# A linear-attention and routed-experts kernel: the first batch in another order, the first two units' x sums in the dense blocks, the balancing in place

## The chip, the cores and the metric

The kernel runs on one core of a Trainium2 chip. Its engines work side by side, each through its own list of instructions in order: PE (TensorE, matmuls), DVE (VectorE), ACT (ScalarE), POOL (GpSimd) and SP (SyncE, which here only issues transfers). They meet through semaphores: an instruction that waits holds up all that stands behind it on its engine. The metric is the time of one execution on the device in microseconds (us), less is better.

## The reference

Eight batches of eight heads, 576 positions, 64 features, in float32. Attention is linear: queries and keys pass a relu and are doubled by a cosine and a sine of the position.

```python
def phi(x, c, s):
    r = np.maximum(x, 0.0)
    return np.concatenate([r * c, r * s], axis=-1)
q_p = phi(q, cos_w, sin_w)
k_p = phi(k, cos_w, sin_w)
kv = np.einsum('bhsf,bhsd->bhfd', k_p, v)
z = np.sum(k_p, axis=2)
num = np.einsum('bhsf,bhfd->bhsd', q_p, kv)
den = np.einsum('bhsf,bhf->bhs', q_p, z)[..., None] + 1e-06
```

The result num / den, as 4608 tokens of 512 features, is the x of a layer of 8 experts. The routing weights P are balanced by eight rounds over rows and columns, and every expert sees every token:

```python
P = np.exp(logits)
for _ in range(8):
    P /= P.sum(1, keepdims=True) + 1e-09
    P /= P.sum(0, keepdims=True) + 1e-09
    P *= N / E
for e in range(E):
    h = np.maximum(x @ w1[e], 0.0)
    out += P[:, e:e + 1] * (h @ w2[e])
```

## The kernel before

The kernel goes through four stages.

**Start and first batch (0 to about 25 us).** POOL issues the loads: queries of batch 0 in two halves (L244, L258), keys, values, the first expert's weights, then batch 1. Between the query loads POOL makes an index row (`iota`) and an identity matrix. From the index row ACT makes the table `cs` of cosines and sines. DVE writes constants, then scales the queries (`prep_q`), PE turns each of them by matmuls with the identity (`turn`), and ACT takes the result out of PSUM. Keys get a relu (`prep_k`), and the sums over positions of the scaled keys come from PE straight (`key_sums`) and go through DVE into `zsel` (`key_sums_made`). `prep_kp` scales keys. `denominators` makes q times z on PE for some heads; after the last head DVE takes the reciprocal and splits it into a high and a low half (`hi`, `hl`). `sums_begun` makes kv on PE, 36 matmuls for a half, `sums_made` copies it to `kv_sb` on ACT. `attend` then, for each of four head pairs (hk), spreads the reciprocals by matmuls (`rb`, copied by ACT), makes the numerators on PE, and DVE multiplies both into `xT`. Between the pairs stand the first matmuls of the first dense block (`first_ps`) and, at L669 to L674, relus and scaled keys of batch 1. `keep_busy(n)` puts n filler matmul blocks of 128 columns on PE.

**Blocks 0 to 6 (to about 165 us).** Tokens are taken in nine blocks of 512. Each has 16 slots: eight matmul groups with w1 (`ffn1`, relu into hT on ACT) and eight halves with w2 (`ffn2`). Into the slots a hand-written table (`at`) puts the attention of the next batches. In block 6, slots 1 and 8, `x_sums_early` makes the four sums of a unit of x (`x_sums`) for units 0 and 1, into buffers of the pool of `k_p`; SP stores three of them in DRAM.

**Blocks 7 and 8 (to about 189 us).** The last dense blocks of the first expert; H takes the place of hT and lies on memory that the attention stage gave back. The sums of units 0 and 1 are read again from DRAM (`x_again`, L1109). Here the balancing starts: `sinkhorn` is a generator, and `balanced(n)` takes n steps of it at given slots. Five steps make a round: row sums and reciprocal; product and column sums; two steps of the second expert's w1 sums (T); a matmul that adds the columns over partitions, and other T steps; reciprocal and the last scaling. Products go to a second buffer `P_exp` that lies expert by expert.

**Seven more experts (to the end).** Their products are made with 7 instead of 8 block products (Strassen's scheme in Winograd's form), on sums of x, w1 and H. A `group` makes four products with w1 for a unit of 2 x 384 tokens, a `Pair` those with w2. The first group loop (e = 1, n = 0) takes in the rest of block 8's `ffn2` and the rest of the balancing (`start_fill`).

What sets the order: `te`, `ve`, `se` are wrappers (InOrder) that keep each engine's instructions about as written; waits come from the tiles that they read and write.

Of the kernel before, what the change touches and what calls it, by code (L numbers as in the profile page):

```python
# [25 lines left out]
def kernel(  # L26
# [128 lines left out]
    def ffn2(hT, w, c0, g, y_ps, fts):  # L155
# [9 lines left out]
        if FT - 1 in fts:  # L165

            if g % 2 == 0 or g < B * TCH // P:
                se.copy(out=acc(g), in_=y_ps)
            else:
                ve.tensor_copy(out=acc(g), in_=y_ps)  # L170
# [9 lines left out]

    NT = N // 2
    TU = 3 * P
    NU = NT // TU
    KH = KT // 2
    FH = FT // 2
    UG = TU // P
    DH = Dm // 2

    def x_part(half, kh, n):
        t0 = half * NT + n * TU  # L190
        return xT[:, kh * KH : (kh + 1) * KH, t0 : t0 + TU]

    x_saved = dram.tile([NU, 3, P, KH * TU], F16, name="x_saved")

    def x_sums(n, ts):

        a11, a12, a21, a22 = (x_part(i, j, n) for i in range(2) for j in range(2))
        s1, s2, s4 = ts
        for out_, in0, in1, op in (
            (s1, a21, a22, ALU.add), (s2, s1, a11, ALU.subtract),  # L200
            (s4, a12, s2, ALU.subtract), (a21, a11, a21, ALU.subtract),
        ):
            ve.tensor_tensor(out=out_, in0=in0, in1=in1, op=op)
            yield
        for i, t in enumerate(ts):
            nc.sync.dma_start(out=x_saved[n, i], in_=t.rearrange("p k t -> p (k t)"))

    with ExitStack() as p1:
# [35 lines left out]
        load(0, 0, "q")  # L244
        gidx = cs_pool.tile([P, C], FP32, name="gidx")
# [4 lines left out]

        ones_sq = cs_pool.tile([P, P], F16, name="ones_sq")
# [6 lines left out]
        load(0, 1, "q")  # L258
        for name in "kv":
            load(0, 0, name)  # L260
            load(0, 1, name)
# [41 lines left out]
        for hh in range(2):  # L303
            ve.tensor_copy(
                out=cs_half[hh * HP : (hh + 1) * HP, :, :, hh],
                in_=cs[hh * HP : (hh + 1) * HP, :, :, 0],
            )
# [8 lines left out]
        C3 = C // 3  # L316

# [6 lines left out]
        with nc.allow_low_precision("sums of zeros and ones"):  # L324
# [11 lines left out]
        ones_col = const.tile([P, 1], FP32, name="ones_col")  # L336
        ve.memset(ones_col[:], 1.0)
        ones_all = const.tile([P, P], FP32, name="ones_all")
        ve.memset(ones_all[:], 1.0)
        eps_row = cs_pool.tile([1, 32], FP32, name="eps_row")  # L340
        ve.memset(eps_row[:], 1e-6 / XS)
# [8 lines left out]
        lent = acc_lo[:, G_LO - 4 : G_LO, :].rearrange("p g d -> p (g d)").bitcast(F16)  # L350
        VA = C * (D + 2)
        v_augs = [
            lent[:, i * VA : (i + 1) * VA].rearrange("p (c d) -> p c d", d=D + 2)
            for i in range(4)
        ]
# [7 lines left out]
        for t in v_augs:  # L363
            ve.memset(t[:, :, D : D + 1], 1.0 / XS)

# [107 lines left out]
        def sums_begun(b, half):  # L473
# [7 lines left out]
            kv_ps = [ps_s.tile([P, 512], FP32, name="small_ps") for hh in range(2)]  # L481
# [75 lines left out]

        def attend(b, hk):

            parts = ((0, 2 * C3), (2 * C3, C))  # L560
            rb_ps = [ps_s.tile([P, 512], FP32, name="small_ps") for _ in parts]
            rb = rb_pool.tile([P, C * HP], FP32, name="rb")
            for i, (c0, c1) in enumerate(parts):
# [8 lines left out]
                se.copy(out=rb[:, c0 * HP : c1 * HP], in_=rb_ps[i][:, 0 : (c1 - c0) * HP])  # L572
            num_ps = [ps_s.tile([P, 512], FP32, name="small_ps") for _ in parts]
# [48 lines left out]
        for hk in range(HK):  # L622
            if hk == 3:
                prep_k(0, 0)
                prep_k(0, 1)
                z_ps = key_sums(0)
                prep_q(0, hk)
                key_sums_made(0, z_ps)
            else:
                prep_q(0, hk)  # L630
            for i in range(3):
                turn(0, hk, i, True)
                keep_busy(3)
        prep_kp(0, 0)
        prep_kp(0, 1)
        denominators(0, range(0, 4))
        keep_busy(8)
        for hk in (2, 3):
            prep_k(0, hk)
        z_ps = key_sums(1)  # L640
        prep_kp(0, 2)
        key_sums_made(1, z_ps)
        prep_kp(0, 3)
        keep_busy(5)
        denominators(0, range(4, 8))
        for half in range(2):
            sums_made(0, half, sums_begun(0, half))
            keep_busy((0, 18)[half])
# [7 lines left out]
        for hk in range(HK):  # L656
            attend(0, hk)
            for kt in ((), (0,), (1,), (2, 3))[hk]:
                for ft, h_ps in enumerate(first_ps):
# [9 lines left out]
            for i in ((), (0,), (1, 2), ())[hk]:  # L669
                prep_k(1, i, i < 2)  # L670
            for i in ((), (0,), (1,), (2, 3))[hk]:
                if i == 3:
                    prep_k(1, i, False)
                prep_kp(1, i)  # L674
# [81 lines left out]
        def x_sums_early(n):  # L756
            ts = [kp_pool.tile([P, C, 2, D], F16, name="k_p") for _ in range(3)]
            for _ in x_sums(n, [
                t[:].rearrange("p c a d -> p (c a d)")[:, 0 : KH * TU].rearrange(
                    "p (k t) -> p k t", k=KH  # L760
                ) for t in ts
            ]):
                pass

        for n in range(2):
            at(B - 2, (1, 8)[n], x_sums_early, n)
# [490 lines left out]
```

## Time and profile before

| what | us |
|---|---|
| median of three executions | 979.27 (979.09 to 979.95) |
| the profiled execution, its own time | 979.95 |
| its span, first to last instruction | 978.2 |
| PE busy | 963.7 |
| DVE busy | 808.2 |
| ACT busy | 565.6 |
| POOL busy | 60.7 |

A line of the timeline has the start in us, the duration in us, the engine, the line of the program (L109 is the wrapper's line, so most instructions have it), the operation, what it writes <- what it reads, the shape, and how many like it stand together (x3; the duration is then that of all). In brackets stands how long the engine was idle before it, and what it waited for. A line of groups ends with busy time in us, mean of one in ns, and idle time before. A line of stretches is told where it is shown.

### The profile page before, as it was taken

What the parts mean: (1) busy time and instruction counts of PE and PEld (TensorE: products, weight loads), DVE (VectorE), ACT (ScalarE), POOL (GpSimd) and SP (SyncE); (2) the same over time, 40 slices, a digit from 0 to 9 for tenths busy, and PEclk for the clock granted to TensorE, in tenths of its full rate; (3) what the DMA queues carried; (4) which work ended last, traced back from release to release, by engine and by line L of the source; (5) the groups of instructions that cost most, each with busy time, mean ns of one, the idle gap of its engine ahead of it and who ended that gap; (6) DMA issues with size and microseconds to landing.
All of it is one profiled execution on the core that took longest, in us unless ns stands there. A gap on an engine that the chain in (4) does not pass through costs nothing.

```text
span 978.2 us, 20250 instructions
## 1 busy us (share of the span) xinstructions
PE 963.7 (99%) x7855; PEld 674.4 (69%) x7855; DVE 808.2 (83%) x1831; ACT 565.6 (58%) x1264; POOL 60.7 (6%) x82
## 2 busy tenths in 40 slices
PE   9999999999999999999999999999999999999997
PEld 6544454557777777777777777777777777777775
DVE  6767774888988888988888888988888888988887
ACT  5766665577776555555555555555555555555551
POOL 6231110010000000000000000000000000000001
PEclk9999999999999999999999999999999999999999
DMA  9999888140103401223103401223103401114435
GB/s 162 187 150 173 149 144 184 32 79 28 48 25 77 84 25 35 65 53 68 40 25 78 83 25 37 64 55 66 40 25 77 83 25 39 36 26 121 126 89 127
DMA packets 81200, 74.72 MB, mean 76 GB/s; under 512 B 33360, under 2 KB 73040, under 8 KB 81104
## 3 DMA queue, kind: packets, MB, share of 16 engines
q0 software_dynamic: 27232, 30.94, 20.6%
q1 hardware_dynamic: 53632, 42.24, 17.6%
q8 instruction: 61, 1.00, 0.4%
q14 instruction: 35, 0.29, 0.1%
q10 hardware_dynamic: 240, 0.26, 0.1%
HBM read 84.30 MB, written 12.98 MB: 99 GB/s over the span
## 4 chain that ended last, share of the span: by engine, by line
PE 93%; DMA 2%; DVE 2%; ACT 1%; POOL 1%; issue 1%; ACTq 0%; POOLq 0%; SPq 0%
PE rows_ps L109 34%; PE h_ps L109 28%; PE p_ps L109 11%; PE copied_ps L109 11%; PE y_ps L109 5%; PE small_ps L109 4%; DMA acc_hi<-q_p 1%; DMA k_ld<-in_k_dram 1%; DMA x_saved<-k_p 1%; ACT hT L109 0%; ACT acc_lo L109 0%; DVE acc_hi L939 0%; POOL hs_last L954 0%; DMA out_dram<-acc_lo 0%; DVE xT L109 0%
## 5 line engine op out<-in xcount | busy, mean ns | idle before, releaser
L939 DVE SCALAR_TENSOR_TENSOR acc_lo<-rows_ps,P_tok,acc_lo 128x512 f32<-128x512 f32 (+1 forms) x322 | 203.9, 643 | 74.9 <-PE rows_ps L109 74.8
L109 PEld LDWEIGHTS <-H 128*128 128x128 f16 x2080 | 203.2, 98 | 82.3 <-issue 1.2
L875 ACT CAST u<-h_ps 128x384 f16<-128x384 f32 x288 | 137.5, 478 | 131.2 <-PE h_ps L109 131.2
L109 PEld LDWEIGHTS <-w1e 128*128 128x128 f16 x1632 | 157.3, 98 | 68.1 <-issue 6.8
L869 DVE CUSTOM_DVE_ANT_0 H<-p_ps,u 128x384 f16<-128x384 f32 x329 | 181.9, 553 | 6.5 <-PE p_ps L109 6.5
L109 PEld LDWEIGHTS <-hs 128*128 128x128 f16 x1500 | 146.6, 98 | 56.2
L109 PE MATMUL p_ps<-xT,T 128*128 128x384 f16 x672 | 164.1, 326 | 1.2 <-DVE H L109 1.0
L109 PE MATMUL h_ps<-S,w1e 128*128 128x384 f16 x672 | 164.1, 326 | 0.6 <-ACT u L109 0.3
L109 PE MATMUL rows_ps<-V,H 128*128 128x256 f16 x1000 | 150.0, 273 | 0.7 <-DVE acc_hi L939 0.7
L109 PE MATMUL h_ps<-xT,w1e 128*128 128x384 f16 (+1 forms) x616 | 149.7, 350 | 0.8 <-ACT H L109 0.8
L109 PE MATMUL rows_ps<-w2e,hs 128*128 128x256 f16 x1000 | 150.0, 273 | 0.0
L907 ACT ACTIVATE H<-h_ps 128x384 f16<-128x384 f32 x144 | 70.6, 490 | 95.1 <-PE h_ps L109 95.1
L109 PEld LDWEIGHTS <-T 128*128 128x128 f16 x1008 | 98.4, 98 | 32.0 <-issue 5.4
L109 PE MATMUL rows_ps<-w2e,H 128*128 128x256 f16 (+1 forms) x568 | 92.5, 285 | 0.0
L888 ACT COPY copied_ps<-h_ps 128x384 f32<-128x384 f32 x144 | 67.5, 469 | 35.5 <-PE h_ps L109 35.5
L898 ACT ACTIVATE H<-copied_ps 128x384 f16<-128x384 f32 x144 | 70.8, 492 | 20.4 <-PE copied_ps L109 20.4
L109 PE MATMUL h_ps<-S,T 128*128 128x384 f16 x336 | 81.8, 324 | 0.6 <-ACT copied_ps L109 0.3
L109 PE MATMUL copied_ps<-xT,w1e 128*128 128x384 f16 x336 | 82.1, 326 | 0.0
L109 PE MATMUL copied_ps<-w2e,H 128*128 128x256 f16 x504 | 75.5, 272 | 0.0
L109 PE MATMUL rows_ps<-V,hs 128*128 128x256 f16 x500 | 75.0, 272 | 0.0
L939 DVE SCALAR_TENSOR_TENSOR acc_lo<-copied_ps,P_tok,acc_lo 128x256 f32<-128x256 f32 x126 | 60.4, 480 | 0.6 <-PE copied_ps L109 0.2
L939 DVE SCALAR_TENSOR_TENSOR acc_hi<-rows_ps,P_tok,acc_hi 128x512 f32<-128x512 f32 (+1 forms) x56 | 41.4, 739 | 20.5 <-PE rows_ps L109 19.7
(144 smaller groups left out, 952.6 us busy)
## 6 DMA issues: line engine op xcount, KB each, us to landing
S<-x_saved SPq DMA_DIRECT2D x114, 192.0 KB, 2.4
out_dram<-acc_lo SPq DMA_DIRECT2D x62, 128.0 KB, 2.4
w1e<-in_moe_w_dram POOLq DMA_DIRECT2D x7, 1024.0 KB, 9.2
w2e<-in_moe_w_dram POOLq DMA_DIRECT2D x7, 1024.0 KB, 9.6
q_ld<-in_q_dram POOLq DMA_DIRECT2D x16, 288.0 KB, 7.0
k_ld<-in_k_dram POOLq DMA_DIRECT2D x16, 288.0 KB, 8.2
v_ld<-in_v_dram POOLq DMA_DIRECT2D x16, 288.0 KB, 9.3
x_saved<-S SPq DMA_DIRECT2D x12, 192.0 KB, 1.8
```

The lines of the kernel that those rows point to most:

```text
L109: i = getattr(self.engine, name)(*args, **kwargs)
L869: latest = ve._custom_dve(TENSOR_ADD_SAT, out=out, in0=ps[:, 0:TU], in1=t[:], s0=FP32_MAX, s1=0.0)
L875: se.copy(out=t[:], in_=ps[:, 0:TU])
L888: se.copy(out=Y[:, 0:TU], in_=X[:, 0:TU])
L898: se.activation(out=h11, in_=Y[:, 0:TU], func=AF.Relu)
L907: se.activation(out=h12, in_=X[:, 0:TU], func=AF.Relu)
L939: ve.scalar_tensor_tensor(out=a, in0=rows, scalar=P_tok[:, g, self.e : self.e + 1], in1=a, op0=ALU.mult, op1=ALU.add,)
```

## The change

In the start, both query loads are issued first, the identity is made between the two key loads, and DVE's constants are written ahead of the queries' scaling; two copies for `cs_half` move behind two of the scaled queries (`halve`). All four queries are scaled ahead of the keys' relus. The scaled keys of pairs 2 and 3 move behind the reciprocals. `attend` is cut in `spread_out` and `numerators`; the second half of kv is made behind the first numerators, in the two banks of `h_ps`. The relus and scaled keys of batch 1 all come behind the last numerators, the two relus on ACT ahead of the first relus into hT.

`x_sums_early` goes. The sums of units 0 and 1 are made by DVE in blocks 7 and 8, in the tiles that the products read, and stored from there; they are not read again.

The balancing works in place in `P_tok`, token by token: product and last scaling write in one run, and the column sums read every eighth value. Its steps are dealt otherwise: 23 in the two blocks (28 before), 17 (12 before) in the first group. The 16 T steps go to rounds 1 to 4, four each. Of block 7's results two, tiles 29 and 31, are copied by DVE instead of ACT.

```diff
-            if g % 2 == 0 or g < B * TCH // P:
+            if g % 2 == 0 or g < (B - 1) * TCH // P:
                 se.copy(out=acc(g), in_=y_ps)
...
         load(0, 0, "q")
+        load(0, 1, "q")
         gidx = cs_pool.tile([P, C], FP32, name="gidx")
...
+        load(0, 0, "k")
         ones_sq = cs_pool.tile([P, P], F16, name="ones_sq")
...
-        load(0, 1, "q")
-        for name in "kv":
-            load(0, 0, name)
-            load(0, 1, name)
+        load(0, 1, "k")
+        for half in range(2):
+            load(0, half, "v")
...
         for hk in range(HK):
+            prep_q(0, hk)
+            if hk == 1:
+                halve()
             if hk == 3:
                 prep_k(0, 0)
                 prep_k(0, 1)
                 z_ps = key_sums(0)
-                prep_q(0, hk)
-                key_sums_made(0, z_ps)
-            else:
-                prep_q(0, hk)
             for i in range(3):
                 turn(0, hk, i, True)
                 keep_busy(3)
         prep_kp(0, 0)
+        key_sums_made(0, z_ps)
+        for hk in (2, 3):
+            prep_k(0, hk)
         prep_kp(0, 1)
         denominators(0, range(0, 4))
+        z_ps = key_sums(1)
         keep_busy(8)
+        key_sums_made(1, z_ps)
+        denominators(0, range(4, 8))
+        sums_made(0, 0, sums_begun(0, 0))
+        keep_busy(20)
         for hk in (2, 3):
-            prep_k(0, hk)
-        z_ps = key_sums(1)
-        prep_kp(0, 2)
-        key_sums_made(1, z_ps)
-        prep_kp(0, 3)
-        keep_busy(5)
-        denominators(0, range(4, 8))
-        for half in range(2):
-            sums_made(0, half, sums_begun(0, half))
-            keep_busy((0, 18)[half])
+            prep_kp(0, hk)
+        spread_out(0, 0)
+        numerators(0, 0)
+        keep_busy(8)
+        spread_out(0, 1)
+        sums_made(0, 1, sums_begun(0, 1, (ps_h[0], "h_ps")))
+        keep_busy(8)
...
         for hk in range(HK):
-            attend(0, hk)
+            if hk > 1:
+                spread_out(0, hk)
+            if hk:
+                numerators(0, hk)
+            if hk == 3:
+                prep_k(1, 0)
+                prep_k(1, 1)
             for kt in ((), (0,), (1,), (2, 3))[hk]:
-                for ft, h_ps in enumerate(first_ps):
+                for ft, h_ps in ((2, first_ps[2]), (3, first_ps[3]), (0, first_ps[0]), (1, first_ps[1])):
...
-            for i in ((), (0,), (1, 2), ())[hk]:
-                prep_k(1, i, i < 2)
-            for i in ((), (0,), (1,), (2, 3))[hk]:
-                if i == 3:
-                    prep_k(1, i, False)
-                prep_kp(1, i)
+        for hk in range(HK):
+            if hk >= 2:
+                prep_k(1, hk, False)
+            prep_kp(1, hk)
         for hk in range(3):
             prep_q(1, hk)
...
-        for n in range(2):
-            at(B - 2, (1, 8)[n], x_sums_early, n)
...
             ve.tensor_tensor(
-                out=P_exp[:].rearrange("p e c -> p c e"), in0=P_tok[:],
+                out=P_tok[:], in0=P_tok[:],
                 in1=rr[:].unsqueeze(2).to_broadcast([P, NG, E]), op=ALU.mult,
             )
...
-            ve.reduce_sum(out=colp[:], in_=P_exp[:], axis=AX.X)
+            ve.reduce_sum(
+                out=colp[:], in_=P_tok[:].rearrange("p c e -> p e c"), axis=AX.X
+            )
...
-                out=P_tok[:].rearrange("p c e -> p e c"), in0=P_exp[:],
+                out=P_tok[:], in0=P_tok[:],
                 scalar=float(N) / float(E) / (XS if it == 7 else 1.0),
-                in1=t2[:].unsqueeze(2).to_broadcast([P, E, NG]),
+                in1=t2[:].unsqueeze(1).to_broadcast([P, NG, E]),
...
-    tw_steps = [[steps_left.pop(0) for _ in range(n)] for n in (2, 3, 4, 3, 4, 0, 0, 0)]
+        tw, tw_steps[1 + i] = w1_steps(w_next, i)
...
-    for n in range(2):
-        x_again(n, xs_first[n])
+    sums_x = x_sums(0, xs_next)
...
-            balanced({1: 3, 4: 5, 8: 5, 13: 5, 17: 5, 22: 5}.get((j - B + 1) * NS + slot, 0))
+            if j == B - 1 and slot:
+                next(sums_x, None)
+            if j == NJ - 1:
+                if slot == 0:
+                    sums_x = x_sums(1, xs_first[1])
+                next(sums_x, None)
+            since = (j - B + 1) * NS + slot - 5
+            if since == -4:
+                balanced(3)
+            elif since >= 0 and since % 5 < 2:
+                balanced((1, 4)[since % 5])
...
-        balanced({3: 1, 4: 1, 5: 1, 6: 2, 11: 1, 12: 1, 13: 1, 14: 2, 19: 1, 20: 1}.get(k_fill, 0))
+        if k_fill % 6 != 1:
+            balanced(1)
```

## The prediction

> **What bounds the kernel now.** I read the page's header, busy line and slices, then busy time by stretches, then the timelines of the two places that the change touches: the first batch (0 to 35 us) and the dense blocks with the Sinkhorn balancing (160 to 205 us).
>
> ```profile
> span 978.2 us, 20250 instructions
> PE 963.7 (99%) x7855; PEld 674.4 (69%) x7855; DVE 808.2 (83%) x1831; ACT 565.6 (58%) x1264; POOL 60.7 (6%) x82
> 24.00:33.00 9.00, 7.45 (x79) 4.45 (x79) 7.10 (x14) 8.41 (x18) 4.43 (x7) 1.00 1.23 205
> 170.00:189.00 19.00, 19.00 (x97) 9.42 (x95) 16.73 (x45) 10.10 (x17) 0.00 (x0) 1.00 0.03 9
> 189.00:205.00 16.00, 14.83 (x83) 7.96 (x82) 12.29 (x26) 9.71 (x21) 1.74 (x2) 1.00 0.40 68
> ```
>
> PE is the bound, so a change pays or costs only where PE stands idle. The last three lines are stretches: length, then busy us of PE, weight loads, DVE, ACT, POOL, then clock (1.00 throughout, so no clock term), DMA. In 24 to 33 ACT is the fullest engine; in 170 to 189 PE has no gap, but DVE is busy 16.7 of 19.
>
> ```profile
> 17.34 0.41 DVE L109 SCALAR_TENSOR_TENSOR hl<-hi,lo,den 96x192 f16<-96x192 f16 x1
> 19.31 0.57 PE L109 MATMUL small_ps<-q_pT,kv_sb 128*64 128x384 f16 x4
> 24.47 1.08 ACT L109 ACTIVATE hT<-h_ps 128x512 f16<-128x512 f32 x2 [1.13 <-PE h_ps L109]
> 25.60 2.09 DVE L109 TENSOR_TENSOR q_p<-q_ld,acc_hi 128x1152 f16<-128x1152 f16 x3
> 26.84 0.67 PE L109 MATMUL small_ps<-ident,q_p 128*128 128x128 f16 x9
> ...
> 161.61 1.39 SPq L206 DMA_DIRECT2D x_saved<-k_p  x3
> 168.81 0.60 ACT L109 ACTIVATE H<-h_ps 128x512 f16<-128x512 f32 x1 [1.72 <-PE h_ps L109]
> 169.46 2.75 PE L109 MATMUL h_ps<-xT,w1e 128*128 128x512 f16 x12 [0.76 <-ACT H L109]
> 201.91 0.48 PE L109 MATMUL p_ps<-xT,T 128*128 128x384 f16 x2 [1.01 <-DVE H L109]
> 202.80 0.48 PE L109 MATMUL h_ps<-S,w1e 128*128 128x384 f16 x2
> ```
>
> These are the marks to compare with: hl (the reciprocals) done at 17.75, the second head pair's numerators at 19.31, batch 1's first scaled query at 25.60, its transposes at 26.84. At 168.81 the first relu into H runs late though its matmul ended near 167.2: H lies on the memory of k_p, and the last of the early x sums is still being stored (in the chain of waits that transfer runs 162.56 to 168.26). PE stands until 169.46. At 201.91 PE waits for a DVE queue full of balancing.
>
> ```profile
> L109 DVE SCALAR_TENSOR_TENSOR P_tok<-P_exp,t 128x288 f32<-128x288 f32 x8 | 5.4, 679 | 0.3
> L109 DVE TENSOR_TENSOR P_exp<-P_tok,rr 128x288 f32<-128x288 f32 x8 | 5.4, 670 | 0.3
> L109 DVE TENSOR_REDUCE colp<-P_exp 128x8 f32<-128x288 f32 x8 | 3.6, 453 | 0.3
> ```
>
> The three operations whose layout changes: two of them write with a stride today, the reduction reads in one run.
>
> **Part 1, the first batch: +1.5 us.** Second query load ahead of the iota on POOL: one issue of 0.77, so the iota and, behind it, the ACT cosine table come 0.75 later (5.04 instead of 4.29). DVE fills that time with its memsets; its first scaling starts when the load lands, 4.7 after issue at 1.30, near 6.05 instead of 6.83. That gain is hidden: the last transposes now stand behind the first key sums on PE, and these wait for the first keys, landed at 10.60. Their issue moves by 0.2 at most (3.38 to about 3.2), bounds -0.3 to 0; I take 0, since the queue is moving data all along.
>
> From there I walk the order of the built new program with today's rows. DVE relus 10.63, key sums on PE to 11.72, turns and fillers to 12.75, denominators 0.44, second key sums 0.66, two fillers 0.43 (beside them the zsel), denominators of heads 4 to 7 end near 14.85 instead of 15.58. Reciprocal 1.35 and two more: hl at 17.02, a gain of 0.73. Now the losses. Behind hl DVE has two scaled keys that were in front (0.68 each), so the first x product starts at 18.4, not 18.70. On PE, between first spread and second numerators, 36 key-sum matmuls (0.66) and two filler blocks (4 x 0.22) are new: spread 17.08, numerators 17.43, filler 17.87, spread 18.30, sums 18.65, filler 19.3, numerators 19.75, against 19.31. The rhythm after that is as before (1.72, 1.58, 1.45 between marks), so the last x product of the batch ends at 24.4 to 24.5 instead of 24.0.
>
> Two piles then stand behind it that used to lie in the gaps between x products. DVE: batch 1's two relus and four scaled keys, 4 x 0.68 + 2 x 0.25 = 3.2, so the first scaled query starts at 27.7, not 25.60, and its transposes at 28.5. ACT: two key relus (0.70 each, 0.59 start to start) ahead of the first relus into hT, which start at 25.0 instead of 24.47; the h banks free later and PE's slots 4 and 5 end at 28.4. Both ways lead to transposes 1.5 to 1.7 after 26.84. From there ACT is gapless up to 32.9 and hands it on; I take +1.5. Low end +0.1 (the 0.44 of the numerators less 0.3, if both piles hide), high end +2.1 (the DVE pile in full). What is late next: weights and loads of batch 2 are paced by DVE's progress, and the stall at 71.7 to 73.9 on a transposed load hangs on loads issued at 51.17 behind DVE, so it moves along and absorbs nothing.
>
> **Part 2, x sums no longer early: -0.9.** Eight DVE sums (0.55 each), six stores, and six reloads of 192 KB leave block 6, where PE was gapless (19.00 of 19.00 from 141 to 160), so their time there is worth nothing; the six stores come back later, unhurried, and the reloads are gone. But H no longer waits for the store: slot 2 starts at 168.53, not 169.46.
>
> **Part 3, the same sums in the dense blocks, and the balancing: +2.4.** DVE gets in 165 to 204: the eight sums, one of them before the softmax weights exist, and two accumulator copies that ACT made (0.60 start to start), one of which waits for PE. Balancing moves from 28 steps in these blocks to 23, leaving 17 instead of 12 for the first group. Price of an iteration: today 172.36 to 175.29, 2.93 from reciprocal to column sums. In place, the product and the last scaling are contiguous: no row has that at 288, the nearest is the 0.453 contiguous reduction, so -0.22 each. The column reduction now reads with a 32 byte stride. Nearest rows: 0.453 if a stride costs a read nothing, 0.453 plus the strided writes' surcharge, 0.67, and twice that surcharge, 0.89. I take 0.67, as a stride of the same kind; then an iteration costs 2.72 (2.50 to 2.94).
>
> [...]
>
> The walk: row sums at 168.3 (the weights' exponential no longer waits behind H), column sums 170.25, three x sums to 171.9, matmul after slot 5 at 172.0; column sums 175.0, four T steps to 175.9; then the reciprocal stands behind the first copy, which waits for slot 11 to end at 177.4; column sums 180.8, copy, T steps, an x sum, 185.5 (slot 20 ends 185.3, PE waits 0.2); three x sums and T steps, 190.7. The first group starts at 188.3, and its fifth column matmul is now in its first fill, at 189.3: PE waits 1.4. After that each matmul of the chain waits for DVE: column sums 194.3, then with four H additions (0.56) and a copy between them 198.9 and 203.35. The mark at 202.80 comes at 204.3, that is +1.5 for parts 2 and 3 together. Bounds: seven iterations at 0.22 more or less, +0.0 to +3.1.
>
> After it the first group ends as before: P_tok is final 1.1 after that mark in both, and gates on POOL (3.12) have 5 us until the first add needs them. The remaining 770 us have the same instructions.
>
> **Sum.** +1.5 +1.5 = +3.0. The profiled execution took 979.95 (span 978.2 and 1.75 around it), the slowest of three and 0.68 over their median 979.27. 979.95 + 3.0 = 982.95 for that execution, 982.3 against the median. Bounds: 979.27 + 0.1 + 0.0 = 979.4 and 979.27 + 2.1 + 3.1 = 984.5.
>
> **Rivals.** (a) The first batch costs nothing: the piles hide in later gaps, or a DMA wait downstream absorbs them. For: PE idles 1.55 in 24 to 33. Against: ACT has no gap there. Then 979.27 + 1.5 = 980.8. (b) DVE keeps up: a strided read costs nothing and PE's fillers cover the rest, parts 2 and 3 near 0. For: DVE has 2.3 idle in 170 to 189, and the new work there, 7 x 0.57 + 2 x 0.60 = 5.2 less the one iteration of 2.9 that moves on, is no more. Against: that iteration lands in the first group, where H additions already made PE wait, and the copies hold DVE for PE. Then 979.27 + 1.5 = 980.8. (c) The strided read costs more than twice the surcharge, say 1.2 in all: 7 x 0.53 more, 986.0. (d) Faster: the reciprocals' 0.73 reaches the end because the DVE pile behind the last x product fits before batch 1's transposes, and the H stall's 0.93 comes on top: 979.27 - 1.7 = 977.6. It decides if the transposes at 26.84 come before 26.8 and the first group's fifth column matmul finds its sums ready. Against it: 3.2 of DVE work with nothing to overlap.
>
> **How the numbers follow.** Mine 0.64 (own range 980.6 to 984.5), (a) 0.12, (b) 0.10, (c) 0.07, (d) 0.07. The range leaves out (d), most of (c) and the tail below: 979.8 to 985.0. A measurement of this kernel tells about 0.2% (1.96 us) from no change, so slower means above 981.2. Slower: 0.85 of mine, a quarter of (a), half of (b), all of (c): 0.69. Faster: most of (d), 0.06. Same: 0.25.
>
> **What would show it.** In the new profile: hl done near 17.0; second numerators near 19.8; batch 1's transposes near 28.4; no ACT wait before PE's slot 2 of the first dense block; colp<-P_tok near 0.67 and the other two near 0.45; PE waits on DVE in front of the column matmuls, the longest just after the first group starts. I am wrong if the transposes come before 27.5, or if those waits add to less than 2 us.

## The result, and the profile after

The changed kernel takes 984.63 us (median of 983.37, 984.23, 985.03 and 985.62), against 979.27 before: a ratio of 1.0053, with a 95% interval from 1.0035 to 1.007. It is slower. A second series of twelve executions on another occasion (below) gave 983.38 against 979.16, 1.0036 (1.0021 to 1.0052), so the loss is 4 to 5 us. The profiled execution is the shortest of the first four, 983.37 with a span of 981.7; the one before took 979.95 with 978.2. The two traces can therefore explain 3.5 us, not the whole difference of the medians.

The header and busy line of the page after, and three stretches of it (length, busy us of PE, weight loads, DVE, ACT and POOL, clock, DMA):

```profile
span 981.7 us, 20241 instructions
PE 965.9 (98%) x7857; PEld 675.0 (69%) x7857; DVE 807.7 (82%) x1833; ACT 564.9 (58%) x1262; POOL 60.5 (6%) x82
24.00:33.00 9.00, 7.16 (x53) 3.66 (x50) 8.55 (x16) 7.69 (x17) 4.28 (x6) 1.00 1.23 206
170.00:189.00 19.00, 18.97 (x92) 8.86 (x91) 16.02 (x41) 8.52 (x15) 0.00 (x0) 1.00 0.09 32
189.00:205.00 16.00, 13.58 (x72) 6.68 (x70) 13.96 (x37) 8.31 (x18) 0.76 (x1) 1.00 0.46 91
```

In 24 to 33 DVE, not ACT, is now the fullest engine (8.55 of 9.00, 7.10 before). In 189 to 205 PE is busy 13.58 us where it was 14.83. The marks further down show that these two stages are where the time went.

The marks of the first batch, from the timeline of the changed kernel:

```profile
17.43 0.41 DVE L109 SCALAR_TENSOR_TENSOR hl<-hi,lo,den 96x192 f16<-96x192 f16 x1
20.58 0.44 PE L109 MATMUL small_ps<-q_pT,kv_sb 128*64 128x384 f16 x4
25.62 1.08 ACT L109 ACTIVATE hT<-y_ps 128x512 f16<-128x512 f32 x2
26.59 1.09 ACT L109 ACTIVATE hT<-h_ps 128x512 f16<-128x512 f32 x2
28.31 0.60 ACT L109 ACTIVATE hT<-h_ps 128x512 f16<-128x512 f32 x1 [0.62 <-PE h_ps L109]
28.65 2.09 DVE L109 TENSOR_TENSOR q_p<-q_ld,acc_hi 128x1152 f16<-128x1152 f16 x3
29.46 0.68 PE L109 MATMUL small_ps<-ident,q_p 128*128 128x128 f16 x9 [0.33 <-DVE q_p L109]
```

The reciprocals are done at 17.84, hardly another time than before (17.75). The second numerators start 1.27 us later, batch 1's transposes 2.62 later.

The start of the dense blocks in the same timeline, and then PE's own timeline from 189 to 209, of which these are all the rows with a wait:

```profile
169.08 0.60 ACT L109 ACTIVATE H<-h_ps 128x512 f16<-128x512 f32 x1 [0.28 <-PE h_ps L109]
169.39 4.48 PE L109 MATMUL h_ps<-xT,w1e 128*128 128x512 f16 x20
```

```profile
192.67 0.39 PE L109 MATMUL copied_ps<-colp,ones_all 128*128 128x8 f32 x2 [1.20 <-DVE colp L109]
196.31 0.39 PE L109 MATMUL copied_ps<-colp,ones_all 128*128 128x8 f32 x2 [0.31 <-DVE colp L109]
201.15 0.39 PE L109 MATMUL copied_ps<-colp,ones_all 128*128 128x8 f32 x2 [0.75 <-DVE colp L109]
205.58 0.39 PE L109 MATMUL copied_ps<-colp,ones_all 128*128 128x8 f32 x2 [0.74 <-DVE colp L109]
```

The first relu into H no longer waits for a store, and PE runs 20 matmuls without a gap where it stood for 0.76. In the first group every column matmul waits for its column sums on DVE: 1.20, 0.31, 0.75 and 0.74, together 3.0 us, against one wait of 1.01 before, for a sum of H.

The three operations of the balancing whose layout changed, from the groups of the dense blocks and first group (count, busy us, mean ns, idle before):

```profile
L109 DVE TENSOR_REDUCE colp<-P_tok 128x8 f32<-128x288 f32 x8 | 5.4, 670 | 0.3
L109 DVE SCALAR_TENSOR_TENSOR P_tok<-P_tok,t 128x288 f32<-128x288 f32 x8 | 3.7, 458 | 0.3
L109 DVE TENSOR_TENSOR P_tok<-P_tok,rr 128x288 f32<-128x288 f32 x8 | 3.7, 458 | 0.3
```

### The profile page after: what moved, and what is told of

It reads as the page before. It is cut to its first block, busy times and chain, and to the rows that moved or that the text cites. A ratio compares the mean times of both kernels' runs of the same rounds, so it can differ in the third digit from the quotient of the medians.

```text
span 981.7 us, 20241 instructions
## 1 busy us (share of the span) xinstructions
PE 965.9 (98%) x7857; PEld 675.0 (69%) x7857; DVE 807.7 (82%) x1833; ACT 564.9 (58%) x1262; POOL 60.5 (6%) x82
## 4 chain that ended last, share of the span: by engine, by line
PE 88%; DMA 4%; DVE 3%; issue 3%; ACT 1%; POOL 1%; POOLq 0%; ACTq 0%; SPq 0%
PE rows_ps L109 33%; PE h_ps L109 26%; PE p_ps L109 11%; PE copied_ps L109 11%; PE y_ps L109 4%; PE small_ps L109 3%; DMA k_ld<-in_k_dram 1%; DMA w2e<-in_moe_w_dram 1%; DMA w1e<-in_moe_w_dram 1%; DMA acc_hi<-q_p 1%; DVE P_tok L109 1%; DVE colp L109 0%; POOL q_ld L202 0%; DVE rs L109 0%; DVE acc_hi L949 0%
## 6 DMA issues: line engine op xcount, KB each, us to landing
out_dram<-acc_lo SPq DMA_DIRECT2D x62, 128.0 KB, 2.4
```

## How the runs are compared

Every experiment left a trace of one execution and 6 to 12 times. Two executions of one kernel can differ by more than the effects sought, so the stages are compared by marks inside each trace, and only then by times. The marks are: the end of the fillers (the 74 matmuls at the start that only keep PE busy, ahead of the first transposes), taken as the start of the matmuls behind them; the end of hl; batch 1's transposes; the exponential of batch 6's weights (155.07 before; the expectations below call these batch 5's, the numbers are those of batch 6); the single matmul that stands ahead of the first group; and the one behind it.

| kernel | fillers end | hl after it | transposes after hl | weights of batch 6 to group | group | last mark to last matmul | median us (before beside it) |
|---|---|---|---|---|---|---|---|
| before | 7.16 | 10.59 | 9.09 | 34.06 | 18.45 | 765.96 | 979.27 |
| changed | 8.27 | 9.57 | 11.62 | 33.54 | 21.20 | 765.53 | 984.63 (979.27) |
| e_after | 8.24 | 9.66 | 11.44 | 33.54 | 21.21 | 765.57 | 983.38 (979.16) |
| e_first | 7.00 | 9.58 | 11.43 | 33.83 | 18.47 | 766.03 | 982.02 (979.56) |
| e_dense | 7.67 | 10.23 | 9.09 | 33.55 | 21.20 | 765.60 | 982.85 (979.56) |
| e_inplace | 7.14 | 10.65 | 9.10 | 33.71 | 18.25 | 766.01 | 979.04 (979.56) |
| e_early5 | 8.07 | 10.20 | 9.10 | 35.42 | 18.46 | 766.03 | 981.85 (979.56) |
| e_copies | 8.12 | 9.58 | 11.43 | 32.99 | 20.03 | 765.82 | 981.87 (979.16) |
| e_deal | 8.02 | 9.57 | 11.60 | 33.74 | 19.06 | 765.72 | 981.13 (979.16) |
| e_piles | 7.92 | 9.58 | 11.11 | 33.54 | 21.20 | 765.57 | 982.90 (979.16) |
| e_banks | 7.06 | 9.79 | 10.13 | 33.54 | 21.20 | 765.50 | 981.70 (979.27) |
| e_both | 6.77 | 9.67 | 11.42 | 33.54 | 18.68 | 765.91 | 981.23 (979.27) |
| e_best | 7.85 | 10.04 | 9.09 | 34.22 | 17.14 | 765.69 | 978.29 (979.27) |
| e_fill60 | 7.29 | 9.90 | 11.43 | 33.54 | 21.20 | 765.54 | 983.04 (979.27) |

What the marks don't hold lies between batch 1's transposes and batch 6's weights: 127.3 to 129.4 us in thirteen of the fourteen traces with no order by kernel (128.2 before, 127.3 in the changed kernel, 129.4 in its repetition), and 131.5 in e_banks, whose PE waited 2.82 there for a transposed load. That is the scatter of the loads, taken up with the repetition below and under the last heading.

## The change in two halves, and the changed kernel once more

**First batch alone.** The kernel before with the new order of loads, preparation, reciprocals and key sums, up to batch 1's first scaled query:

```diff
         load(0, 0, "q")
+        load(0, 1, "q")
...
+        spread_out(0, 0)
+        numerators(0, 0)
+        keep_busy(8)
+        spread_out(0, 1)
+        sums_made(0, 1, sums_begun(0, 1, (ps_h[0], "h_ps")))
...
-                prep_kp(1, i)
+        for hk in range(HK):
+            if hk >= 2:
+                prep_k(1, hk, False)
+            prep_kp(1, hk)
```

> The kernel before with the new first batch alone; x sums, their early place and the balancing stay as they were. Theory: the first batch is a cost of its own. In the trace of the full change the transposes of batch 1 came 2.6 us later (26.84 to 29.46) and 0.95 of that was taken up again at the wait for a transposed load near 72 to 75, so 1.7 us should remain at the end: 981.0 us. Rival: most of the 2.6 belongs to the one profiled execution, in which TensorE stayed at half speed until about 7.2 us and not 4.75, so that the first evictions came 1.1 later; then an execution with the earlier switch shows transposes near 28.4 and what is left behind the wait near 72 is some 0.6 or less: 979.9 us. Second rival, the first batch costs nothing: 979.3 us.

**The other half alone.** No early x sums; sums in the dense blocks, balancing in place with the new dealing, two copies on DVE; the first batch as before:

```diff
-            if g % 2 == 0 or g < B * TCH // P:
+            if g % 2 == 0 or g < (B - 1) * TCH // P:
...
-        for n in range(2):
-            at(B - 2, (1, 8)[n], x_sums_early, n)
...
+            if j == B - 1 and slot:
+                next(sums_x, None)
```

> The kernel before with the other half of the change alone: no early x sums, their sums in the dense blocks, in-place balancing with the new dealing of steps, and the two copies on VectorE; the first batch stays as it was. Theory: the missing stall ahead of the second slot gives 0.9 back and the denser VectorE queue costs 2.7 in the first group, together +1.8 us: 981.1 us, with TensorE waiting ahead of the column matmuls of the first group by 1.2, 0.3, 0.75 and 0.75. Rival: the first batch costs nothing in the end and this half carries all of it, +5.4 us: 984.6 us. Second rival: VectorE has room and the only effect is the stall that goes: 978.4 us.

**The changed kernel, unedited, again.**

> The changed kernel once more, unedited, to have its time beside the three that follow and a second look at its first microseconds. Theory: TensorE's change from half to full speed comes at another moment in each execution (4.75 us in the profile before, about 7.2 in the profile after), and the new first batch hands the delay of the fillers on to its end (transposes of batch 1 at 29.46 with the fillers ending at 8.27; at 28.0 with an end near 7.0), so the times spread over 3 us or more, median 983 to 985 us. Rival: the late first evictions belong to the new order of the loads, and the transposes are at 29.4 whenever the fillers end.

Measured: the first batch 982.02 (979.52 to 985.43), ratio 1.0023 (1.0013 to 1.0033); the other half 982.85 (980.88 to 984.8), 1.0032 (1.002 to 1.0045); both 983.38, 1.0036. The two halves add up to 5.75 us by their medians against 4.2 to 5.4 for the whole, so both cost, and neither rival that puts everything on one half stands. By the marks the second half costs 33.55 + 21.20 against 34.06 + 18.45, which is +2.24, less some 0.4 behind the last mark: +1.9, just below the low end of its timed interval; what makes the median longer than that is not located.

The first batch shows the rival's mechanism, but not its conclusion. In the trace of e_first the fillers end at 7.00 and hl is done at 16.58; in the changed kernel they end at 8.27 and hl is done at 17.84. The distance is the same, 9.57 to 9.67, in seven of the eight traces with the new first batch and 74 fillers (9.79 in e_banks, answered under the fillers). In the changed kernel the keys are ready first, and PE comes to the key sums later, behind fillers and transposes without a gap (first DVE's row, then PE's):

```profile
10.44 0.52 DVE L109 TENSOR_SCALAR k_ld<-k_ld 128x576 f16<-128x576 f16 x2
11.79 0.73 PE L109 MATMUL small_ps<-cs_half,k_ld 128*64 128x2 f16 x36
```

What moves the fillers is TensorE's speed. The same stretches in both profiles, for the fillers alone (the number behind PE's busy time counts the fillers that touch 0.4 us; first of the kernel before, then of the changed one):

```profile
4.00:4.40 0.40, 0.40 (x6) 0.40 (x5) 0.00 (x0) 0.00 (x0) 1.00 1.13 190
5.20:5.60 0.40, 0.40 (x11) 0.40 (x9) 0.00 (x0) 0.00 (x0) 1.00 0.89 92
6.40:6.80 0.40, 0.40 (x11) 0.40 (x9) 0.00 (x0) 0.00 (x0) 1.00 1.29 190
```

```profile
5.20:5.60 0.40, 0.40 (x7) 0.40 (x5) 0.00 (x0) 0.00 (x0) 1.00 1.19 202
6.40:6.80 0.40, 0.40 (x7) 0.40 (x5) 0.00 (x0) 0.00 (x0) 1.00 0.98 133
7.20:7.60 0.40, 0.40 (x10) 0.40 (x9) 0.00 (x0) 0.00 (x0) 1.00 1.11 170
```

The same matmuls become faster between 4.4 and 5.2 in one execution, between 6.8 and 7.2 in the other, while the granted clock reads 1.00 throughout. In the kernel before it is 0.108 us from one filler to the next ahead of the change (13 more of them in the 1.4 us from 3.0 on) and 0.057 behind it (14 more in the 0.8 us from 6.0 on). Nothing ahead of this in PE's work differs. The thirteen traces with 74 fillers scatter likewise: these end anywhere from 6.77 to 8.27, at 7.14 to 8.07 in the five with the old first batch and at 6.77 to 8.27 in the eight with the new one, so the order of the loads doesn't set it. The trace of e_after alone could not have told this, since its fillers ended late again (8.24); e_first and e_both, with early ends, do, with transposes at 28.01 and 27.86. What does set the moment, no run shows.

The old first batch takes up half of that: its hl stands 10.6 behind an early end of the fillers and 10.0 to 10.2 behind a late one, since it waits for loads as well (in the kernel before PE stands 0.19 for the keys' relu, at 10.99). The new one, with both query loads in front, hands it on in full. Over the traces with 74 fillers and untouched order, batch 1's transposes come at 26.84 to 27.37 with the old first batch (mean of five 27.01) and at 27.86 to 29.46 with the new one (mean of six 28.83): +1.8 us. The execution of e_first that was profiled is one of the short ones (980.13), and its +1.17 at the transposes is not typical.

The repetition of the changed kernel says the same of the scatter downstream. Its marks in the table are those of the first trace within 0.2, and still its span is 1.9 longer, 983.6. The timeline of e_after, on ACT and on PE:

```profile
61.87 0.68 ACT L109 ACTIVATE k_ld<-k_ld 128x576 f16<-128x576 f16 x1 [3.51 <-DMA k_ld<-in_k_dram]
```

```profile
63.46 0.47 PE L109 MATMUL small_ps<-hl,acc_hi 96*128 96x192 f16 x3 [2.36 <-ACT rb L109]
```

One key load of batch 2 landed late, ACT stood 3.51 in front of its relu (1.29 in the first trace), and PE 2.36. No line of the kernel differs.

## Inside the first batch

**Batch 1's preparation back between the x products.**

```diff
-            if hk == 3:
-                prep_k(1, 0)
-                prep_k(1, 1)
...
+            for i in ((), (0,), (1, 2), ())[hk]:
+                prep_k(1, i, i < 2)
+            for i in ((), (0,), (1,), (2, 3))[hk]:
+                if i == 3:
+                    prep_k(1, i, False)
+                prep_kp(1, i)
```

> The changed kernel with batch 1's relus and scaled keys back between the first batch's x products, as before; all else of the new first batch stays. Theory: the 3.2 us of VectorE work behind the last x product set the first scaled query of batch 1, so with it in the gaps the transposes come 1.0 to 1.8 us earlier for the same end of the fillers and the time falls by 0.5 to 1.5 us. Rival: the work delays the x products by as much as it is earlier itself, the transposes stay within 0.4 us, and the loss of the first batch lies in the later second numerators and in the relus on ScalarE.

**The same, and the four x product banks in their old order.**

```diff
-                for ft, h_ps in ((2, first_ps[2]), (3, first_ps[3]), (0, first_ps[0]), (1, first_ps[1])):
+                for ft, h_ps in enumerate(first_ps):
```

> The changed kernel with batch 1's preparation back between the x products (as in e_piles) and, besides, the four banks of the first x products taken in their old order, so that the two shared with the following slots are filled and emptied first. From hl to the transposes of batch 1 it was 9.1 us before, 11.4 in the changed kernel and 11.1 with the preparation moved back alone. Theory: of the rest, 1.2 is the later second numerators and the other 0.9 the order of the banks, which keeps the next slot's matmul waiting for the last relus; with the old order 10.1 to 10.3 us. Rival: the order of the banks is of no account and ScalarE's or VectorE's queue sets the transposes: 11.1 us again.

The piles were a miss: with both of them gone, DVE's and ACT's, it is 11.11 from hl to the transposes instead of 11.43, a gain of 0.32, within the 0.4 of the rival (the relus on ScalarE, where it looked for the rest, are gone here too). DVE is early now (scaled query at 26.39), but PE isn't there yet. With the bank order added it is 10.13, inside the forecast. PE's rows for slots 4 and 5, in the changed kernel and in e_banks, and ACT's timeline of e_banks show why:

```profile
27.25 1.89 PE L109 MATMUL h_ps<-xT,w1e 128*128 128x512 f16 x8 [1.01 <-ACT hT L109]
```

```profile
25.26 1.89 PE L109 MATMUL h_ps<-xT,w1e 128*128 128x512 f16 x8
```

```profile
24.61 1.09 ACT L109 ACTIVATE hT<-h_ps 128x512 f16<-128x512 f32 x2 [1.13 <-PE h_ps L109]
25.58 1.09 ACT L109 ACTIVATE hT<-y_ps 128x512 f16<-128x512 f32 x2
26.54 1.24 ACT L109 ACTIVATE hT<-h_ps 128x512 f16<-128x512 f32 x2
```

Here the two banks of h_ps are emptied first, and slots 4 and 5, which need them, have their own relus follow at 26.54 without a gap. In the changed kernel (lines above) y_ps goes first at 25.62, h_ps second at 26.59, and the next h_ps relu comes only at 28.31, behind PE's wait of 1.01. So of the 2.34 us that the new first batch adds between hl and the transposes, 0.32 is the pile alone, 0.98 the order of the banks once the pile is gone, and 1.04 is left, which no run takes out; the second numerators, which stand 2.74 behind hl instead of 1.56, are 1.18 later in every trace with the new order. The shares depend on this order of undoing: in the changed kernel PE waits 0.33 for the scaled query at 29.46 after it has waited 1.01 for the bank, so the old order of the banks with the pile left in place, which was not run, could hardly have gained anything. The median falls with each step, 982.90 with the preparation back and 981.70 with the banks as well, but the intervals of the ratios, 1.0031 (1.0017 to 1.0045) and 1.0022 (1.0006 to 1.0038), overlap.

**Fewer fillers.**

```diff
-        for _ in range(74):
+        for _ in range(60):
```

> The changed kernel with 60 fillers instead of 74 ahead of the first transposes. In four profiles of the new first batch hl was done 9.57 to 9.66 us after the last filler, whether these ended at 7.00 or at 8.27. Theory: in late executions the fillers themselves hold the first transposes, whose query is scaled by 6.8; with 60, which end near 6.1 even at half speed, hl is done by 16.4 to 16.9 in any execution, and the median falls by 0.5 to 1.2 us. [...]

In the execution that was profiled the 60 fillers ran from 1.15 to 7.29, and the 6.1 of the theory was wrong as an end: it is how long they took. hl was done at 17.19, later than the 16.9 of the theory. Here the load of the keys is what holds it, as DVE's and PE's rows show:

```profile
10.78 0.53 DVE L109 TENSOR_SCALAR k_ld<-k_ld 128x576 f16<-128x576 f16 x2 [0.58 <-DMA k_ld<-in_k_dram]
11.14 0.73 PE L109 MATMUL small_ps<-cs_half,k_ld 128*64 128x2 f16 x36 [0.25 <-DVE k_ld L109]
```

hl is therefore 9.90 behind the fillers. In e_banks, whose 74 fillers ended early (7.06), the keys' relu waited for its load too (1.02), and the distance is 9.79. Fewer fillers thus hand the start over to the next limit, which stands close behind. The median is 983.04, ratio 1.0032 (1.0019 to 1.0045) against 1.0036 for 74 fillers: the 0.3 us is in the expected direction and inside the intervals. That the fillers' end sets hl where they end late is shown by the traces; that fewer fillers help is not shown.

## Inside the dense blocks and the first group

**The balancing in place, alone.**

```diff
-                out=P_exp[:].rearrange("p e c -> p c e"), in0=P_tok[:],
+                out=P_tok[:], in0=P_tok[:],
...
-            ve.reduce_sum(out=colp[:], in_=P_exp[:], axis=AX.X)
+            ve.reduce_sum(
+                out=colp[:], in_=P_tok[:].rearrange("p c e -> p e c"), axis=AX.X
+            )
```

> The kernel before with one edit: P_tok is scaled in place, so the product and the last scaling write in one run and the column reduction reads with a stride; the dealing of the steps stays. Theory: 0.670 and 0.679 become 0.458 each and 0.453 becomes 0.670, so an iteration is 0.21 us shorter on VectorE; in the first group of the grouped stage, where TensorE waited 1.0 for a sum of H behind the balancing, 0.2 to 0.7 us come back: 978.8 us, and the balancing is no cause of the loss. Rival: the strided read, on the way from product to column matmul, costs more than the shorter writes give: 979.5 to 980 us.

979.04 us, ratio 0.9991 (0.9983 to 1.0), group 18.25 instead of 18.45. The layout is no cause of the loss; the 0.20 in the group says that it pays a little, and the interval of the time reaches up to no change.

**The copies back on ACT**, **the old dealing**, and **both**:

```diff
-            if g % 2 == 0 or g < (B - 1) * TCH // P:
+            if g % 2 == 0 or g < B * TCH // P:
```

> The changed kernel with the two accumulator copies of the dense blocks back on ScalarE. Theory: on VectorE they cost 0.68 each and one of them waits 1.60 for TensorE with the balancing queued behind it, so without them VectorE is some 2 us earlier at the group's start; the wait of 1.20 ahead of the first column matmul goes and the later ones shrink: group from its start mark to its end mark 19.5 to 20.3 instead of 21.20, time 1 to 2 us under the changed kernel. Rival: the copies fall into idle time of VectorE and the two more copies on ScalarE hold the relus: no gain, 21.2 again.

```diff
+    tw_steps = [[steps_left.pop(0) for _ in range(n)] for n in (2, 3, 4, 3, 4, 0, 0, 0)]
...
+            balanced({1: 3, 4: 5, 8: 5, 13: 5, 17: 5, 22: 5}.get((j - B + 1) * NS + slot, 0))
...
+        balanced({3: 1, 4: 1, 5: 1, 6: 2, 11: 1, 12: 1, 13: 1, 14: 2, 19: 1, 20: 1}.get(k_fill, 0))
```

> The changed kernel with the old dealing of the balancing, 28 steps in the dense blocks and 12 left for the first group, and the weight sums dealt as before; x sums, copies and the in-place balancing stay. Theory: what costs in the first group is the iteration more that it holds, 17 steps for 12; with 12 the group takes some 19 instead of 21.20, and the dense blocks take the iteration with waits of under 1 us: time 1 to 2 us under the changed kernel. Rival: VectorE is the limit of the dense blocks with the x sums in them, the waits only move to the column matmuls there, and the sum of both stretches stays within 0.4 us.

> The changed kernel with both the old dealing of the balancing and the two copies back on ScalarE; new first batch, x sums in the dense blocks and the in-place balancing stay. From batch 5's softmax weights to the end mark of the first group it was 52.5 us before, 54.7 in the changed kernel, 53.0 with the copies back and 52.8 with the old dealing. Theory: the two are one queue on VectorE, and with both gone the x sums are free: 52.0 to 52.4 us, time 0.4 to 0.8 us under that of the old dealing alone (981.13). Rival: the x sums cost as well, 52.8 us again.

From batch 6's weights to the end of the group: 52.51 us before, 54.74 in the changed kernel (54.74 to 54.75 in all six traces with its dense half), 53.02 with the copies back, 52.80 with the old dealing, 52.22 with both. The times follow, 981.87, 981.13 and 981.23, but the last one misses its forecast of 0.4 to 0.8 under 981.13; that the last two are alike while the stretch differs by 0.58 is within their scatter. What PE waited for on DVE from 165 to 214, in the changed kernel and with the old dealing:

```profile
PE copied_ps L109 <- DVE colp L109: 3.0, 4, 1.2
```

```profile
PE p_ps L109 <- DVE H L109: 0.8, 1, 0.8
PE copied_ps L109 <- DVE colp L109: 0.5, 1, 0.5
```

One copy does harm beyond its length, as DVE's timeline of the changed kernel shows:

```profile
177.47 0.28 DVE L109 TENSOR_TENSOR T<-w1e,T 128x256 f16<-128x256 f16 x1
179.35 0.69 DVE L109 COPY acc_lo<-rows_ps 128x512 f32<-128x512 f32 x1 [1.60 <-PE rows_ps L109]
179.96 0.20 DVE L109 RECIPROCAL t<-copied_ps 128x8 f32<-128x8 f32 x1
```

DVE stands 1.60 for PE's slot with the next reciprocal behind it, whose column sums had long been broadcast (178.15). Each of the two causes removes most of the loss alone because they are one queue: 1.72 and 1.94 of 2.23, 2.52 together. With both gone the stretch is 0.29 shorter than before and 0.26 longer than with the layout alone (51.96): that is what moving the eight x sums from block 6 into the dense blocks costs on balance. It is a balance of two things, since with the layout alone PE still waits 0.42 for H ahead of slot 2, and with both gone it doesn't; the theory's "free" is nearly right for the balance only.

**The early x sums, three slots earlier.**

```diff
-            at(B - 2, (1, 8)[n], x_sums_early, n)
+            at(B - 2, (1, 5)[n], x_sums_early, n)
```

> The kernel before with one number changed: the second unit's early x sums stand behind slot 5 of block 6 instead of slot 8, so that their stores begin some 2.6 us earlier. Theory: the stall ahead of slot 2 of the first dense block is only the late store of those sums, whose memory H takes over (0.76 on TensorE, 0.93 in the sequence of slots); it goes without moving any work into the dense blocks: 978.4 us, first relu into H without a wait for a transfer. Rival: the scratch tiles are those of the scaled keys, three of four, and asking for them earlier makes VectorE wait for the first unit's stores, so that the scaled keys of batch 7 come late and the 0.9 is lost again there: 979.3 us or more.

981.85 us, 1.0028 (1.0018 to 1.0039): the rival. H no longer waits for a store, as the theory had it, but more is lost ahead of that. DVE's timeline of e_early5:

```profile
155.61 0.55 DVE L109 TENSOR_TENSOR k_p<-xT 128x768 f16<-128x768 f16 x1
158.23 0.56 DVE L109 TENSOR_TENSOR k_p<-k_p,xT 128x768 f16<-128x768 f16 x1 [2.08 <-DMA x_saved<-k_p]
159.53 0.56 DVE L109 TENSOR_TENSOR k_p<-xT,k_p 128x768 f16<-128x768 f16 x1 [0.74 <-DMA x_saved<-k_p]
```

Four tiles of k_p don't hold two units' three sums while the first three are being stored, and a store took 7.0 us to land here (median of the six; 6.5 for the same six in the kernel before, where the second unit asked for the tiles later). DVE stood 2.8 and PE 2.1 behind it. The old place, slot 8, was late for H and slot 5 is too early for the tiles; the slots between were not tried. The change to the dense blocks is one way out of that.

**Dealing the other way, for a faster kernel.** The kernel before, in place, with 33 of 40 steps in the dense blocks and 7 in the group:

```diff
-    tw_steps = [[steps_left.pop(0) for _ in range(n)] for n in (2, 3, 4, 3, 4, 0, 0, 0)]
+    tw_steps = [[steps_left.pop(0) for _ in range(n)] for n in (2, 2, 3, 2, 2, 2, 3, 0)]
...
-            balanced({1: 3, 4: 5, 8: 5, 13: 5, 17: 5, 22: 5}.get((j - B + 1) * NS + slot, 0))
+            balanced({1: 3, 4: 5, 8: 5, 12: 5, 16: 5, 20: 5, 23: 5}.get((j - B + 1) * NS + slot, 0))
...
-        balanced({3: 1, 4: 1, 5: 1, 6: 2, 11: 1, 12: 1, 13: 1, 14: 2, 19: 1, 20: 1}.get(k_fill, 0))
+        balanced({4: 1, 5: 1, 6: 1, 7: 2, 12: 1, 13: 1}.get(k_fill, 0))
```

> The kernel before with the in-place balancing and a denser dealing the other way: 33 of the 40 steps in the dense blocks, one iteration per four slots, 7 in the first group (before 28 and 12, the changed kernel 23 and 17), the weight sums dealt two or three to an iteration; x sums and first batch stay as before. Theory: VectorE has room in the dense blocks and none in the first group, where TensorE still waits 1.0 for a sum of H; the group goes from 18.25 us to 17.4 to 17.6, the dense blocks lose 0.3 at most, and the time is 0.9 to 1.4 us under the kernel before: 977.8 to 978.3 us. Rival: an iteration (2.7 us and its weight sums) doesn't fit into four slots of 0.87, the column matmuls wait there, and the stretch from batch 5's weights to the group's end mark stays at 52.0 us as with the in-place balancing alone.

The two stretches of e_best, from batch 6's weights to the group and the group itself:

```profile
154.24:188.46 34.22, 33.70 (x197) 16.25 (x196) 23.19 (x60) 18.21 (x37) 0.23 (x1) 1.00 0.44 107
188.46:205.60 17.14, 16.90 (x93) 8.83 (x93) 11.16 (x27) 11.54 (x25) 3.64 (x3) 1.00 0.36 63
```

The group takes 17.14 us, 1.3 less than before and less than the 17.4 to 17.6 of the forecast, with PE busy 16.90 of it; the dense blocks take 34.22, 0.5 more than with the layout alone, where 0.3 at most was forecast. Together 51.36 against 52.51. The median is 978.29 against 979.27, 1.0 us as expected, but the interval of the ratio, 0.9993 (0.9978 to 1.0008), holds no change too. The stage is shown to be 1.15 us shorter in one trace; that the kernel is faster is likely and not shown.

## Why the prediction was right

The time came out as forecast, slower, +5.4 and +4.2 in two series against +3.0: the second, 983.38, lies inside the sum's own bounds, the first, 984.63, just above their upper end of 984.5. Both halves cost, as the sum had it, by the marks 1.8 and 1.9, or 3.7 together; the 0.5 to 1.7 by which the medians are longer still is not located. Some of the steps were right in size for another reason than the one given. By its own steps:

- **Reciprocals earlier by 0.73 (hl at 17.02).** The gain is there, with another size each time. The step that failed is "these wait for the first keys, landed at 10.60": in the changed kernel the keys' relu started at 10.44 and PE reached the key sums at 11.79, behind fillers and transposes. The keys hold it, by 0.2 to 0.3 in e_banks and e_fill60, only where the fillers end early. hl follows the fillers, and is 1.2 earlier than before with an early change of speed (16.58 in e_first against 17.75) and about 0.4 with a late one (17.84 against 18.27 in e_early5). On the mean of the traces it is 0.6 earlier (17.30 in eight, 17.92 in five), so that the 0.73 came out near it is luck. "So no clock term" is where this was lost: it was read off the granted clock, 1.00, while the fillers themselves showed a change of speed, from 0.108 to 0.057 us each.
- **Losses behind hl.** Second numerators 2.73 after hl by the forecast, 2.74 measured; transposes 11.4 after it by the forecast, 11.43 measured. Of the two ways that were said to lead there, DVE's is right: the first scaled query was to start 10.7 after hl and starts 10.8 after it (28.65). The other arrives nearly as late, which is why taking the pile out gains 0.32 alone, but not for the reason given. It was put down to ScalarE's two key relus; without them the first relu into hT stands 7.76 behind hl in e_piles, and 7.78 with them. The order of the four banks, which the walk did not look at, is what delays the next slots, by 1.0.
- **Part 1 in sum, +1.5.** +1.8 by the means of the transposes. The step that the stall near 72 absorbs nothing holds in the mean: from the transposes to batch 6's weights it is 128.0 with the old first batch and 128.1 with the new one (eight traces, without e_banks). In single traces PE's wait there is 0 to 2.8 whatever the kernel.
- **Part 2, -0.93.** Slot 2 did come 0.93 earlier against slot 0 (169.46 before, 170.25 in the changed kernel, with slot 0 moved by 1.72). Of that 0.42 was gone by the start of the group, since two column matmuls, at 182.80 and 187.51, waited 0.1 to 0.2 each for their sums on DVE and ran longer than the others (0.39 us against 0.28). The eight sums themselves were rightly put down as room on DVE.
- **Part 3.** Operations: 0.67 forecast and 0.670 measured for the strided reduction, about 0.45 and 0.458 for the other two. The first wait was forecast at 1.4 and took 1.20, the copy's wait for PE was in the walk and took 1.60. The term that was too small is the group: the mark at 202.80 was to come at 204.3 and came at 206.58, or 204.86 without what the first batch had added: +2.1 for parts 2 and 3 there, not +1.5. At the end it is +1.8, because the rest of the kernel takes 0.4 less (765.53 for 765.96), and "the remaining 770 us have the same instructions" missed that. The 0.4 lies at two single matmuls: 0.15 at one that stands 4.8 behind the group, and 0.28 at one near 677 in the kernel before, where PE's next weight load stands idle for 0.35 with nothing in the profile that it waits for. The six traces with the whole dense half run through both places; before, e_first, e_inplace, e_early5 and e_both stand at both. The cause stays open.
- **Rivals.** (a), a free first batch, falls with e_first. (b), DVE that keeps up, falls with the waits of 3.0 us; its remark that the two copies hold DVE for PE was the better half. (c), a read at 1.2, falls with 0.670. (d), faster, asked for transposes before 26.8, and none of the new first batches reached that.

## What to carry over

Where the loss of a stage is a queue on an engine that isn't the bound, several causes each seem to own nearly all of it (1.72 and 1.94 of 2.23 here), and where two queues arrive side by side, each seems to own next to nothing (0.32 for the pile, 1.30 for pile and banks): undo them together before sizing one. Compare small edits by distances between marks within a trace, which agreed to 0.01 us over six traces of one stage, before comparing times that scatter by 3 us. When a load is moved forward, ask what stands next on that path: here it was the kernel's own fillers, and their end differs by 1.5 us between executions, and where they end early the load of the keys stands next.

## What the hardware showed that was not expected

- The step of PE's fillers from 0.108 to 0.057 us each came at 4.4 to 5.2 us in one execution, and a like one at 6.8 to 7.2 in another, with the same instructions ahead of it; the granted clock in the profile's rows says 1.00 on both sides of it.
- Between 36 and 155 us PE's wait for a load or a transposed load differed between executions of unchanged code: 0.92 for the transposed query in the changed kernel, none in its repetition, where it waited 2.36 behind a late key load instead.
- A store of 192 KB on SP's queue took 7.0 us to land in block 6 of e_early5 and 6.5 in the kernel before (medians of six), beside two 1 MB loads of expert weights; the profile of the kernel before has 1.8 as the median of the twelve later stores of that size.
